# Unit 5's q and k in an attention and feed-forward kernel: transposed by a DMA instead of by TensorE

## The chip, the cores and the metric

The kernel runs on one NeuronCore of a Trainium2 chip. The metric is the device time of one execution in microseconds (us), taken as the median of several runs. The engines are TensorE (PE; its weight loads are listed as PEld), VectorE (DVE), ScalarE (ACT), GpSimd (POOL) and SyncE (SP). SP only issues DMAs here. The DMAs that SP issues run in queue q1, those that POOL issues in queue q0, those of ACT in q10; all share the core's 16 DMA engines.

## The reference

What is computed is attention with normalised q and k, followed by a feed-forward block with a leaky ReLU. Cut to what matters:

```python
batch, n_heads, seq, head_dim = 8, 12, 448, 64
n_tokens, d_model, d_ff = 3584, 768, 2048

def rmsnorm(x, g):
    rms = np.sqrt(np.mean(x * x, axis=-1, keepdims=True) + 1e-06)
    return x / rms * g

q_n, k_n = rmsnorm(q, g_q), rmsnorm(k, g_k)
scores = np.matmul(q_n, k_n.transpose(0, 1, 3, 2)) / np.sqrt(64)
scores = scores - np.max(scores, axis=-1, keepdims=True)
attn = np.exp(scores)
attn = attn / (np.sum(attn, axis=-1, keepdims=True) + 1e-09)
attn_out = np.matmul(attn, v)

x = attn_out.transpose(0, 2, 1, 3).reshape(3584, 768)
h = x @ w_in
out = np.maximum(0.01 * h, h) @ w_out
```

## The kernel before

**Units.** The 96 heads are worked off as 24 units of four heads, three units for a batch (`NU = 24`, `NQ = 3`, `QH = 4`). Each unit holds 4 x 448 rows of q, k and v, laid out on 128 partitions as `[128, 2, 7, 64]`.

**What one unit passes through**, with the lines that the profile names:

- `load` (L152): two DMAs of SP bring q and k as float32 into `raw` (three buffers each). `load_v` (L155): POOL brings v as float16 (four buffers).
- The squares, on POOL (`prep_sqp`, L179) for units 2 to 8, on ACT (L175) for the others; their sums on DVE (`prep_ssq`, L186); the inverse root as two small ACT instructions (`prep_rinv`, L191 and L192); the product with it on DVE, one instruction for q and one for k, into the float16 tile `n16`, of which there is one buffer (`prep_norm`, L198).
- The transpose of `n16` into `qkT` (three buffers), of which there are two kinds. With `prep_tr` (L205 to L212), TensorE multiplies seven 128 x 128 blocks with the identity (L210) into a PSUM bank, and DVE copies the bank to `qkT`; the copy of q multiplies by g on the way (`vcopy`, L822), the copy of k is plain (L824). With `prep_trd` (L215), one DMA of SP transposes q and k together, and DVE multiplies q by g in place afterwards (`prep_g`, L182).
- The scores (`qk`, L228): seven steps of four 64 x 64 matmuls over 448 columns, each step into a pair of PSUM banks. The step's exponential is one ACT instruction of 128 x 896 (`ex`, L243), which empties the pair. The first step also gives the unit's shift: a maximum on DVE (`shift_max`, L257 and L259), one matmul that spreads it over the partitions (`shift_mm`, L276) and two small DVE instructions (L277, L287).
- The product with v (`pv`, L403), the column sums (`zcol`, L340), some of whose terms DVE adds up first (`add_e`, L325), the copy out of PSUM (`pv_out`, L353 on DVE or L355 on ACT), the inverse of the sums on ACT (`zcol_ln`, L361, and `zcol_inv`, L366), which four small DMAs of SP spread over the partitions (L371), and the product with it (`xmul`, L381).

**The feed-forward block.** The two weight matrices are loaded by POOL's queue at the beginning (L131 for w_in; L134 for w_out, two DMAs of 1.5 MB each). While the units run, TensorE works off a queue of feed-forward items between a unit's groups of scores: products with w_in (`moe1`, L425), whose leaky ReLU is ACT's L419, and with w_out (L471 and, in a form with fewer products, L535). DVE forms the sums of weights for that form (`weight_sum`, L499).

**Order.** The order is written by hand and recorded as it stands (`manual_schedule`); no scheduler moves anything. Units 0 to 2 are written out one step after the other. From unit 3 on, a loop goes over the units `u` and, in each, over four groups `d`. A group issues its scores and exponentials, gathers a list of jobs, and then `fill` issues as many feed-forward items as a table says (`PLAN`), one job after each item, and the remaining jobs behind the last item. So a job's place in the list sets its place in each engine's queue. For unit u the groups do, for other units:

- group 0: `load(u + 4)`; up to u = 5 `prep_sqp(u + 3)`; up to u = 4 `load_v(u + 3)`. From u = 5 the load of v stands behind a one-element POOL copy that reads `qkT` of unit u + 1 (`gate_t_of`, L293).
- group 1: the sums of squares for u + 2.
- group 2: `prep_rinv` and `prep_norm` for u + 2, and, from u = 4, `prep_trd` for u + 2, so that unit 6 is the first that a DMA transposes.
- units 4 and 5 are transposed by `prep_tr`, in group 1 of unit 3 and in group 0 of unit 4.

A transpose of unit u + 2 must be read out of `n16` before the norm of unit u + 3 writes it, one unit later. The multiply by g of a unit that a DMA transposed is a job of group 1 in the unit before (`prep_g(u + 1)`, from u = 5).

**PSUM.** The eight banks are handed out from a list of free ones. Until unit 5, scores take pairs among banks 4 to 7 (two pairs), and single banks among 0 to 3 serve the feed-forward items, the sums and the transposes. From unit 5 all banks are shared, and a group takes three pairs.

Of the kernel before, what the change touches and what calls it, by code (L numbers as in the profile page):

```python
# [18 lines left out]
def kernel(  # L19
# [18 lines left out]
    NU = B * NQ  # L38
# [192 lines left out]
    def qk(u, steps):  # L231
        st[u]["sT"] = []
        for t in steps:
            sT = slot()
            score(u, t, (sT[:, 0], sT[:, 1]))
            st[u]["sT"].append((t, sT))
# [16 lines left out]
    def shift_max(u):  # L253
        s = st[u]
        sT = s["sT"][0][1]
        s["spare"] = sT[:, 0]
        nc.vector.tensor_reduce(s["spare"][:, 511:512], sT[:, :, 0:S], axis=AXL.XY, op=ALU.max)  # L257
        s["dg"] = small.tile([P, P], FP16, tag="dg", name="dg")
        nc.vector.tensor_tensor(s["dg"], ident16, s["spare"][:, 511:512].broadcast_to([P, P]), op=ALU.mult)  # L259
# [4 lines left out]
    def shift_mm(u):  # L264
        s = st[u]
        peak = s["spare"][:, 510:511]
        own = s.get("own")
        if own is not None:
            pb = own[:, :, S:S + 64]
            for x in range(2):  # L270
                nc.tensor.matmul(pb[:, x], onesp, s["dg"][:, 64 * x:64 * x + 64], start=True, stop=True)
            peak = small.tile([P, 1], FP32, tag="peak", name="peak")
            nc.vector.tensor_reduce(peak, pb, axis=AXL.XY, op=ALU.max)
        elif u > 0 and "zc" in st[u - 1]:
            pb = st[u - 1]["zc"][:, 2 * P:3 * P]
            nc.tensor.matmul(pb, onesp, s["dg"], start=True, stop=True)  # L276
            nc.vector.tensor_reduce(peak, pb, axis=AXL.X, op=ALU.max)  # L277
        else:
            if "pb" not in s:
                shift_bank(u)  # L280
            pb = s["pb"]
            nc.tensor.matmul(pb[:, 0:P], onesp, s["dg"], start=True, stop=True)
            nc.vector.tensor_reduce(peak, pb[:, 0:P], axis=AXL.X, op=ALU.max)
            if u >= 3:
                drop(pb)
        s["eb"] = small.tile([P, 1], FP32, tag="eb", name="eb")
        nc.vector.tensor_scalar(s["eb"], peak, -1.0, DELTA, op0=ALU.mult, op1=ALU.add)  # L287
# [44 lines left out]
    def zcol(u):  # L332
        s = st[u]
        s["zc"] = aux()
        ets = z_tiles(u)
        for i, e in enumerate(ets):
            for y in range(2):
                for a in range(2):
                    c = 32 * (2 * y + a)
                    nc.tensor.matmul(s["zc"][c:c + 32, 0:HS], onesr, e[:, a, HS * y:HS * y + HS],  # L340
                                     start=(i == 0), stop=(i == len(ets) - 1))

    def pv_slot(u):
        s = st[u]
        s["pslot"] = slot()
        s["pv"] = [s["pslot"][:, r] for r in range(2)]
        pv(u)
# [25 lines left out]
    def xmul_sb(u):  # L373
        xmul_pool(u, nc.vector)
# [76 lines left out]
    def flush(keep=0):  # L451
        kept = [p for p in pend if keep and (p[0] in (s1, s2, s3, s4) or hasattr(p[0], "waits") or keep == 5 and hasattr(p[0], "copies"))]
        now = [p for p in pend if p not in kept]
        pend[:] = kept
        for fn, args in now:
            fn(*args)
# [344 lines left out]
    def tripled(u):  # L801
        return 5 <= u < NU - 2

    def narrow(u):
        return 3 <= u < NU - 1
# [43 lines left out]
    with tc.manual_schedule():  # L849
# [208 lines left out]
        for u in range(3, NU):  # L1058
            for d in range(4):
                if u == 5 and d == 0:  # L1060
                    shared.append(u)
                if d > 0 or u > 3:
                    qk(u, (TRIPLES if tripled(u) else STEPS)[d])
                    if d == 0:
                        shift_max(u)
                        flush()
                        if u in (5, 6):
                            xmul_sb(u - 2)
                        if narrow(u - 1):
                            pv_slot(u - 1)  # L1070
                            zcol(u - 1)
                            shift_mm(u)
                            pv_out(u - 1)
                            if u < NU - 1:
                                zcol_ln(u - 1)
                                zcol_inv(u - 1)
                        else:
                            zsum_slot(u - 1)
                            pv(u - 1)
                            shift_mm(u)  # L1080
                            zinv(u - 1)
                    ex(u, 2)
                    if d == 0 and u == NU - 1:
                        zcol_ln(u - 1)
                if d == 2 and (u == 3 or ADDED.get(u, 0) > 3) and u < NU - 1:
                    add_e(u)
                    if u > 4:
                        xmul_sb(u - 1)
                jobs = []

                def job(fn, *args):
                    jobs.append(lambda: fn(*args))

                if d == 0:
                    if u == 3:
                        prep_norm(4)
                        gate(4)
                    elif not narrow(u - 1):
                        xmul(u - 1)
                    if u + 4 < NU:  # L1100
                        job(load, u + 4)
                    if u < 5:
                        load_v(u + 3)
                    if u < 6:
                        prep_sqp(u + 3)
                    if 5 <= u < NU - 3:
                        gate_t_of(u + 1)
                        load_v(u + 3)
                if d == 1 and narrow(u - 1) and not 5 <= u < 8 and ADDED.get(u, 0) < 4:
                    if u % 6 == 2:  # L1110
                        behind.append(u - 1)
                    elif u < NU - 2:
                        xmul_pool(u - 1)
                if u == NU - 1:
                    if d == 1:
                        job(zcol_inv, u - 1)
                if fed(u, d) and u > 3:
                    push(u // NQ - 1)
                if (u, d) in ((3, 1), (4, 0)):
                    for ti in range(2):  # L1120
                        prep_tr(u + 1, ti, VV)
                if u + 2 < NU:
                    if d == 1:
                        if ADDED.get(u) == 3 and u > 3:
                            job(lambda u: (prep_ssq(u + 2), add_e(u)), u)
                        else:
                            for ti in range(2):
                                job(prep_ssq, u + 2, ALL, (ti,))
                if d == 1 and 5 <= u < NU - 1:
                    job(prep_g, u + 1)  # L1130
                if u + 2 < NU:
                    if d == 2:
                        job(prep_rinv, u + 2)
                        if u == 6:
                            job(xmul_sb, u - 1)
                        for ti in range(2):
                            job(prep_norm, u + 2, ALL, (ti,))
                        if u > 3:
                            job(prep_trd, u + 2)
                if d == 1 and 4 <= u < 8:  # L1140
                    job(weight_sum, u - 4, 0)
                if d == 0 and 5 <= u < 9:
                    job(weight_sum, u - 5, 1)
                if d == 1 and u == NU - 2:
                    job(xmul_sb, u - 1)
                    job(add_e, u)
                if u == NU - 2 and d == 0:
                    for n, tile_ in ((1, (raws, "rq", 3)), (2, (raws, "rk", 3)), (3, None), (4, (prep_p, "sq", 3))):
                        job(win_sum, n, 1, tile_)
                    for n in (3, 1, 2, 4):  # L1150
                        job(x_sum, LATE, n)
                if u == NU - 1 and d == 3:
                    job(add_e, u)
                    job(xmul_sb, u - 1)
                if d == 3 and 6 <= u < NU - 3:
                    for ti in range(2):
                        job(prep_sq, u + 3, ALL, (ti,))
                if st[u]["sT"]:
                    n = 1 if d == 1 and u % 6 == 2 else 0
                    jobs[n:n + 1] = [also(lambda: ex(u), *jobs[n:n + 1])]  # L1160
                fill(u, d, jobs)
# [39 lines left out]
```

## Time and profile before

| | |
|---|---|
| median of 3 runs | 409.06 us (408.88 to 409.59) |
| the profiled execution | 408.8 us, of which the span of the profile is 406.9 us |
| granted TensorE clock | 1.00 throughout |
| TensorE busy | 396.7 us (97%) |
| VectorE busy | 311.3 us (76%) |
| ScalarE busy | 303.9 us (75%) |
| GpSimd busy | 70.6 us (17%) |
| DMA transposes (L215) | 18, median 4.0 us from issue to landing, the longest 6.6 us |
| transposes on TensorE through `prep_tr` (L210) | 42 matmuls, between 33.7 and 56.6 us |
| w_out (L134) | issued at 30.8 and 33.3 us, landed 25.5 to 31.4 us later |
| shift of units 3 and 4 begins (L257) | at 38.93 and 54.11 us |

The span runs from the first to the last instruction of the profile; the time of an execution holds a little more. A line of the timeline gives an instruction's start and length in us, its engine, its source line, its operation, what it writes and reads, and in square brackets how long its engine stood idle before it and what ended that. Busy shares are averages over a start, 21 units and an end of different kinds. PE's ends are modelled, so that consecutive matmuls overlap a little in the timeline. The DMA view lists packets, megabytes and the time that the packets took as a share of 16 engines, for each queue in a stretch of time.

### The profile page before, as it was taken

Reading aid. Unit: us, or ns where it says so; the run is one execution under the profiler, and the core shown is the slowest. Engines: PE = TensorE matmul, PEld = TensorE weight load, DVE = VectorE, ACT = ScalarE, POOL = GpSimd, SP = SyncE. Lnnn points to the kernel's source line nnn. Section 1 sums busy time; section 2 is a strip of 40 time slices with the busy share of each in tenths; the row PEclk is TensorE's granted clock in tenths of the full one; section 3 lists DMA queues with packets and bytes.
Section 4 is the critical chain, followed back from the end, with each engine's and each line's share of the span. In section 5 each row is a group of like instructions: output and inputs, shape, how many; then the busy total and the mean of one; then the engine's idle time right before and its main releaser. Section 6 shows DMA issues by size and latency. Waiting matters only on the chain.

```text
span 406.9 us, 9527 instructions
## 1 busy us (share of the span) xinstructions
PE 396.7 (97%) x3876; PEld 225.0 (55%) x3876; DVE 311.3 (76%) x482; ACT 303.9 (75%) x474; POOL 70.6 (17%) x88
## 2 busy tenths in 40 slices
PE   8999999999999999999999999999999999999996
PEld 7665454555455544555455544555455557559963
DVE  5888999988879665886679756787679889567672
ACT  5998877788977699778978689868987667743600
POOL 1787432200120200120011200020002200000000
PEclk9999999999999999999999999999999999999999
DMA  6999999999455887478563795777732470022023
GB/s 197 276 235 251 240 235 246 236 223 213 96 156 110 239 216 117 135 198 192 137 159 66 226 218 116 187 178 170 177 72 49 122 169 0 20 68 79 0 57 99
DMA packets 72527, 62.87 MB, mean 154 GB/s; under 512 B 36389, under 2 KB 67621, under 8 KB 72485
## 3 DMA queue, kind: packets, MB, share of 16 engines
q1 hardware_dynamic: 61888, 50.08, 46.3%
q0 software_dynamic: 10272, 11.80, 18.8%
q8 instruction: 30, 0.49, 0.5%
q10 hardware_dynamic: 324, 0.39, 0.3%
q14 instruction: 13, 0.10, 0.1%
HBM read 45.61 MB, written 11.01 MB: 139 GB/s over the span
## 4 chain that ended last, share of the span: by engine, by line
PE 87%; DVE 2%; issue 0%; DVEq 0%
PE banks L425 29%; PE banks L535 25%; PE banks L228 9%; PE banks L471 8%; PE banks L669 6%; PE banks L403 6%; PE banks L340 3%; PE banks L276 1%; DVE banks L257 1%; DVE ost L542 1%; PE banks L210 0%; PE banks L433 0%; DVE xt L412 0%; DVE dg L259 0%; PE banks L313 0%
## 5 line engine op out<-in xcount | busy, mean ns | idle before, releaser
L243 ACT ACTIVATE et<-banks,eb 128x896 f16<-128x896 f32 x168 | 160.6, 1008 | 22.8 <-PE banks L228 22.1
L425 PE MATMUL banks<-xt,win 128*128 128x448 f16 x612 | 122.2, 353 | 0.0
L425 PEld LDWEIGHTS <-win 128*128 128x128 f16 x612 | 57.6, 98 | 56.2 <-issue 6.9
L419 ACT ACTIVATE gt<-banks 128x448 f16<-128x448 f32 x104 | 55.2, 551 | 9.1 <-PE banks L425 7.6
L186 DVE TENSOR_REDUCE ssq<-sq 128x14 f32<-128x896 f32 (+2 forms) x49 | 50.3, 1058 | 0.8 <-ACT sq L175 0.8
L228 PE MATMUL banks<-qkT 64*64 64x448 f16 x672 | 49.0, 361 | 1.6 <-DVE qkT L824 0.8
L535 PEld LDWEIGHTS <-sa 128*128 128x128 f16 x352 | 33.4, 98 | 26.1 <-issue 5.1
L535 PE MATMUL banks<-tw,sa 128*128 128x384 f16 x264 | 46.9, 326 | 0.0
L542 DVE TENSOR_TENSOR ost<-banks,ost 128x384 f32<-128x384 f32 x55 | 30.4, 553 | 13.2 <-PE banks L535 12.3
L257 DVE TENSOR_REDUCE banks<-banks 128x1 f32<-128x896 f32 x24 | 26.3, 1098 | 15.1 <-PE banks L228 11.1
L403 PE MATMUL banks<-et,vt 64*64 64x448 f16 x672 | 36.9, 349 | 0.0
L535 PEld LDWEIGHTS <-gt 128*128 128x128 f16 x264 | 25.5, 98 | 18.2 <-issue 1.7
L198 DVE TENSOR_TENSOR n<-rq,rinv 128x896 f16<-128x896 f32 (+2 forms) x25 | 33.1, 1328 | 1.9 <-ACT rinv L192 1.9
L471 PE MATMUL banks<-wout,gt 128*128 128x384 f16 x192 | 33.7, 326 | 0.0
L228 PEld LDWEIGHTS <-qkT 64*64 64x64 f16 x672 | 16.6, 105 | 29.1 <-issue 21.8
L535 PE MATMUL banks<-wout,gt 128*128 128x384 f16 x176 | 32.4, 326 | 0.0
L293 POOL COPY gate_t<-qkT 128x1 f16<-128x1 f16 x16 | 4.0, 251 | 152.3 <-DMA qkT<-n 152.3
L198 DVE TENSOR_TENSOR n<-rk,rinv 128x896 f16<-128x896 f32 (+2 forms) x26 | 26.1, 1012 | 0.0
L403 PEld LDWEIGHTS <-vt 64*64 64x64 f16 x672 | 20.0, 107 | 10.0
L471 PEld LDWEIGHTS <-gt 128*128 128x128 f16 x192 | 18.0, 98 | 13.7 <-issue 2.9
L325 DVE TENSOR_TENSOR ea<-et 128x896 f16<-128x896 f16 x14 | 10.0, 714 | 18.2 <-ACT et L243 18.2
L381 POOL TENSOR_TENSOR xt<-x,rz 128x896 f16<-128x896 f32 x8 | 16.6, 2077 | 32.3 <-DMA rz<-zs 26.0
(109 smaller groups left out, 492.4 us busy)
## 6 DMA issues: line engine op xcount, KB each, us to landing
rq<-in_q_dram SPq DMA_DIRECT2D x24, 448.0 KB, 5.2
rk<-in_k_dram SPq DMA_DIRECT2D x24, 448.0 KB, 6.0
out_dram<-ost SPq DMA_DIRECT2D x52, 192.0 KB, 3.0
rz<-zs SPq DMA_DIRECT2D x80, 112.0 KB, 3.6
vt<-in_v_dram POOLq DMA_DIRECT2D x24, 224.0 KB, 5.3
win<-in_moe_w_in_dram POOLq DMA_DIRECT2D x8, 384.0 KB, 14.7
wout<-in_moe_w_out_dram POOLq DMA_DIRECT2D x2, 1536.0 KB, 28.4
out_dram<-ost SPq DMA_DIRECT2D x4, 96.0 KB, 2.1
```

The source lines that it names most:

```text
L186: nc.vector.tensor_reduce(buf(u, "ssq")[:, ti, :, c[0]:c[1]], buf(u, f"sq{ti}")[:, :, c[0]:c[1]], axis=AXL.X, op=ALU.add)
L198: nc.vector.tensor_tensor(buf(u, "n16")[:, ti, c[0]:c[1]].rearrange("p s a d -> p a s d"), src[:, :, c[0]:c[1]], buf(u, "rinv")[:, ti, :, ...
L228: nc.tensor.matmul(banks[a][64 * r:64 * r + 64, 0:S].rearrange("p (t x) -> p t x", t=NS), kT(u, r, a, t), qT(u, r, a), start=True, stop=True)
L243: nc.scalar.activation(s["et"][:, t], sT[:, :, 0:S], AF.Exp, bias=s["eb"], scale=1.0)
L257: nc.vector.tensor_reduce(s["spare"][:, 511:512], sT[:, :, 0:S], axis=AXL.XY, op=ALU.max)
L403: nc.tensor.matmul(s["pv"][r][64 * a:64 * a + 64, 0:S], vts[u % NV][64 * r:64 * r + 64, a, t], s["et"][64 * r:64 * r + 64, t, a], start=(t ...
L419: nc.scalar.activation(dst, src, AF.Prelu, bias=0.0, scale=1.0, alpha=0.01)
L425: nc.tensor.matmul(hps[:, 0:S], win16[:, kt // 2, kt % 2, ts(ft, P)], xt[:, kt // 2, kt % 2], start=(kt == 0), stop=(kt == KT - 1))
L471: nc.tensor.matmul(op2[:, 0:HC], gt[:, ft, ds(col(t), P)], wout16[:, ft, ds(HC * half, HC)], start=(i == 0), stop=(i == FT - 1))
L535: nc.tensor.matmul(bank[:, 0:HC], a[:, f], b[:, f], start=(first and f == 0), stop=(f == HF - 1), skip_group_check=not first)
L542: nc.vector.tensor_tensor(dst, g[name][:, 0:HC], src, op=ALU.add)
L669: nc.tensor.matmul(bank[:, HX * i:HX * i + HX].rearrange("p (t x) -> p t x", t=NS), w, x[:, kt], start=start, stop=(kt == HK - 1), skip_gr ...
```

## The change

Unit 5 is no longer transposed by TensorE in group 0 of unit 4. Its transpose is issued as a DMA, as a last job of group 2 of unit 3, and its multiply by g becomes the first job of group 2 of unit 4. The later units keep their order.

```diff
@@ -1116,7 +1116,7 @@
                 if fed(u, d) and u > 3:
                     push(u // NQ - 1)
-                if (u, d) in ((3, 1), (4, 0)):
+                if (u, d) == (3, 1):
                     for ti in range(2):
                         prep_tr(u + 1, ti, VV)
@@ -1126,7 +1126,7 @@
-                if d == 1 and 5 <= u < NU - 1:
+                if d == (2 if u == 4 else 1) and 4 <= u < NU - 1:
                     job(prep_g, u + 1)
                 if u + 2 < NU:
                     if d == 2:
                         job(prep_rinv, u + 2)
                         if u == 6:
                             job(xmul_sb, u - 1)
                         for ti in range(2):
                             job(prep_norm, u + 2, ALL, (ti,))
-                        if u > 3:
-                            job(prep_trd, u + 2)
+                        job(prep_trd, u + 2)
```

In the order of the instructions, TensorE loses 14 transposes (L210, two banks of seven) between unit 4's L276 and the next L425. DVE loses one L822 and one L824 of 128 x 896 there, and gains one L182 of 128 x 896 ahead of unit 6's norm. SP gains one transpose between the loads of unit 7 and the four copies of unit 3's L371. On ACT, the small pair L191 and L192 for unit 6 moves behind the second L419 of its group. The functions that the change calls in new places stand unchanged:

```python
def prep_g(u):
    nc.vector.tensor_scalar(buf(u, "qkT")[:, 0], buf(u, "qkT")[:, 0], gcol, None, op0=ALU.mult)

def prep_trd(u):
    nc.sync.dma_start_transpose(
        out=buf(u, "qkT").rearrange("p t s x -> p (t s) x"),
        in_=buf(u, "n16").rearrange("p t s a d -> p (t s a d)"))
```

## The prediction

> **What bounds the kernel now.** I read the page first, then the chain of waits, then the timeline of units 3 to 5, then the DMA view of short stretches.
>
> ```profile
> span 406.9 us, 9527 instructions
> PE 396.7 (97%) x3876; PEld 225.0 (55%) x3876; DVE 311.3 (76%) x482; ACT 303.9 (75%) x474; POOL 70.6 (17%) x88
> DMA  6999999999455887478563795777732470022023
> ```
>
> TensorE is busy for 97% of the span, so whatever it no longer does, or waits for, shows in the end. The DMA digits are 9 or more from slice 2 to slice 10 (10 to 102 us): the change puts its transfer into the fullest stretch. In the chain, the transposes that go are one entry:
>
> ```profile
> 56.06 0.78 PE banks L210 x14
> 56.85 1.14 PE banks L425 x6
> 57.98 0.56 PE banks L228 x8
> ```
>
> What stands around it in the timeline (start, length):
>
> ```profile
> 55.84 0.23 PE L276 MATMUL banks<-dg,onesp 128*128 128x128 f16 x1
> 56.44 0.36 ACT L361 ACTIVATE zs<-banks 128x224 f32<-128x224 f32 x1 [2.15 <-DVE banks L277]
> 57.12 0.99 ACT L243 ACTIVATE et<-banks,eb 128x896 f16<-128x896 f32 x1
> 57.51 0.68 DVE L822 TENSOR_SCALAR qkT<-banks,gcol 128x896 f16<-128x896 f16 x1
> 58.10 0.61 DVE L824 COPY qkT<-banks 128x896 f16<-128x896 f16 x1
> ```
>
> L276 makes unit 4's shift, and ACT starts on unit 4 only after it. This is ahead of the transposes and does not move. The first exponential ends at 57.12 + 0.99 = 58.11.
>
> **TensorE's part.** Removed: 14 transposes, 0.78 us of the chain. The six matmuls of L425 then end near 57.2. The scores behind them (L228 x8) need two pairs of PSUM banks: one is emptied by DVE's L353 (56.51, 1.08 us: 57.59), the other by that exponential, at 58.11. Today the second four scores begin near 58.2, so they gain about 0.1 us, and the rest of the 0.78 us becomes a wait. ACT has no room to follow either: from 56.44 to 66.43 its timeline shows one idle moment, 0.17 us. Gain on the path: 0.1 us, at most 0.78. Two PSUM banks less are taken in turn, so the built program uses other banks in units 4 and 5 and the same ones from unit 6; none of the new waits names a late reader, so I cost it at 0.
>
> **DVE's and ACT's part.** Removed: L822 and L824, 57.51 to 58.63, 1.12 us. Added: one multiply L182, 0.44 us (median of its 18; 1.09 where POOL's squares run beside it, but POOL idles from 61.5 to 69.4). ACT's small pair for unit 6 (L191, L192, 0.5 us) comes behind the second prelu of the group instead of ahead of it, so unit 6's norm can start at about 64.8, against 64.92 now: cost 0. DVE reaches the new multiply near 64.0: it is four adds behind, and the last add waits for an exponential that ends at 63.30.
>
> **The DMA's part.** Added: one transpose of 448 KB on SP's queue, when unit 5's norm ends (53.00 + 1.08 = 54.1). It stands ahead of four copies that are issued at 57.24. Issuing the next unit's took SP 2.63 us:
>
> ```profile
> 57.24 2.58 SPq L371 DMA_DIRECT2D rz<-zs  x4
> ...
> 67.07 2.63 SPq L215 DMA_TRANSPOSE qkT<-n  x1
> ```
>
> So 54.1 + 2.63 = 56.8, before 57.24: SP delays nobody, with 0.4 us to spare. No POOL gate follows this transpose. In q1's rings, though, the four copies (needed at 68.45 by L381) and unit 8's loads now lie behind it.
>
> What is late if it lands late: the multiply, and behind it in DVE's order the norm of unit 6 and the maximum of unit 5, on which TensorE's shift waits.
>
> ```profile
> 64.92 1.08 DVE L198 TENSOR_TENSOR n<-rq,rinv 128x896 f16<-128x896 f32 x1
> 65.92 1.08 DVE L198 TENSOR_TENSOR n<-rk,rinv 128x896 f16<-128x896 f32 x1
> 67.11 1.10 DVE L257 TENSOR_REDUCE banks<-banks 128x1 f32<-128x896 f32 x1
> 68.65 0.23 PE L276 MATMUL banks<-dg,onesp 128*128 128x128 f16 x1
> ```
>
> From a landing: 0.05 to start, 0.40 for the multiply, 2.08 for the norms (64.92 to 67.00), 0.07 to L257, so L257 starts 2.6 us after it. Today it starts at 67.11. Loss = landing - 64.5, and 0 before that. TensorE's own path (scores of unit 5 right after the multiply, then pv, 1.32 us, and 0.3 to 0.4 of sums) is shorter than DVE's.
>
> When does it land? The trace has no transpose against a full software queue; each later one has its rings nearly to itself. I bound it from the rows of four stretches: 50 to 54, 57 to 61, 64.2 to 67 and 58 to 71.1 us, one after the other (packets, MB, share of time):
>
> ```profile
> q0 software_dynamic: 328, 0.50, 68.1%
> q1 hardware_dynamic: 325, 0.55, 43.0%
> ...
> q0 software_dynamic: 543, 0.83, 114.5%
> ...
> rz<-zs SPq DMA_DIRECT2D x4, 112.0 KB, 7.4
> ...
> q0 software_dynamic: 358, 0.30, 66.1%
> q1 hardware_dynamic: 361, 0.42, 51.8%
> ...
> q0 software_dynamic: 1444, 1.63, 71.6%
> ```
>
> q0 carries w_out and v, q1 is SP's. Where both have work they move the same number of packets, 328 to 325 and 358 to 361, whatever their sizes. From 57 to 61 q1 moves nothing although L371 was issued at 57.24: a first packet takes some 3.8 us to appear beside a full q0. So unit 5's transpose begins at 54.1 + 3.8 = 57.9, and then q0 still has 1444 packets. A transpose alone, in the stretch 92.4 to 95:
>
> ```profile
> q1 hardware_dynamic: 1846, 0.52, 107.5%
> ```
>
> some 1,800 small packets in 2.6 us, 710 per us. Lower bound: q0 yields; 57.9 + 2.6 + 0.5 (last packet to landing: issued at 91.32, landed 4.0 later) = 61.0, no loss. Upper side: packet for packet, the transpose is not through until q0 has run out. Those 1444 packets take at least 1.63 MB / 211 GB/s (q0 alone from 57 to 61) = 7.7 us and at most 1444 / 128 per us (358 in 2.8 us) = 11.3 us. The other 348 packets take 0.5 us, the landing 0.5. Sum: 66.6 to 70.2, and up to 71 if the slowest ring decides, as q0 itself ran until 71.0. I take packet for packet, because both rows with two busy queues show it, and 69.0, a little above the middle, since the small packets are not free to q0 either. Loss 69.0 - 64.5 = 4.5 us; the 0.1 us of TensorE is lost in that wait.
>
> [...] The rows of two plain transfers agree with one record a turn; no row of this case shows a transpose's turn.
>
> **Sum.** This execution: 406.9 us of span, 1.9 us around it, 408.8. Plus 4.5: span 411.4, 413.3. The median of the runs, 409.06, lies 0.26 above the profiled one: 413.5.
>
> **Rivals.**
>
> First, the transfer is hidden: the transpose gets more than one packet a turn and lands before 64.5. For it: about 10 us between norm and multiply, and a transpose alone needs 4.0. Against it: the equal counts above. Then only TensorE's 0.1 us stays: 409.0, not slower. It decides from one point, landing at 64.5.
>
> Second, the change does what it removes: all of 0.78 us comes off the path, 408.3. It would need an early landing and the second pair of banks free by 57.4, while the exponential that empties it ends at 58.11 and hangs on L276, which does not move. Even whole, it is 0.19%.
>
> Third, half late: two or three packets a turn, landing 65.3 to 66.5, loss 0.8 to 2.0: 410 to 411.
>
> Fourth, later than my upper side: the engines wait for each other within the transpose, or TensorE loses its clock in the gap. All stretches of this trace show the granted clock at 1.00, so no row prices it; with a landing at 71.5 the loss is 7, 416. [...]
>
> **How the numbers follow.** Packet for packet with a loss of 2 to 7 us: 0.58, own range 411.1 to 416. Hidden: 0.24. Whole gain: 0.08. Half late: 0.05. Later still: 0.05. About 0.2% (0.8 us) is what a measurement of this kernel tells from no change. Slower 0.58 + 0.05 + 0.05 = 0.68; of the hidden case 0.22 is within the bound and 0.02 beyond, as is the whole gain: same 0.22, faster 0.10. The range starts at the hidden case, 408.8, and ends at 416; outside it lie the whole gain and the last case, some 0.15.
>
> **What would show it.** Right: DVE idle ahead of L182 near 64 us, ended by the DMA qkT<-n; that transpose landing 12 us or more after issue, against 4.0 to 6.6 of the others; TensorE idle near 66.6 and again ahead of the next L276; from there every line later by the same amount. In any case: no L210 after 47 us and a wait of L228 near 57.6. Wrong: L182 near 64 without idle time, and L276 of unit 5 at 68.6 or before. Equal packet counts on q0 and q1 from 58 us on would prove the step on turns, 1,800 packets on q1 while q0 moves a few hundred would refute it.

## The result and the profile after

The changed kernel takes 416.32 us (416.04 to 416.52, four runs) against 409.03 for the kernel before in the same comparison: 1.0177 times as long, 95% interval 1.0162 to 1.0191. The forecast was 413.5 and its range ended at 416.0, so the direction was right and the loss was 7.3 us where 4.5 had been forecast. The profiled execution is one of 416.39 us. (Further down, three executions that were disturbed as a whole, of `a1_gate_v`, of `b1_no_tr` and of the kernel before, at 2,253, 803 and 1,405 us, are left out.)

First the page of the changed kernel: its span, the busy times, and the chain of waits by engine and line.

```profile
span 414.4 us, 9499 instructions
PE 398.1 (96%) x3862; PEld 224.9 (54%) x3862; DVE 309.5 (75%) x481; ACT 303.8 (73%) x474; POOL 70.5 (17%) x88
...
PE 83%; DMA 4%; DVE 2%; issue 0%; DVEq 0%
```

TensorE has 14 instructions fewer and is busy for 1.4 us longer. A DMA now holds 4% of the chain. The chain in order of time, from 54 us, says which one:

```profile
54.11 0.18 PE banks L403
54.29 16.95 DMA qkT<-n
71.24 0.03 issue
71.26 0.46 DVE qkT L182
71.73 0.14 issue
71.86 0.59 PE banks L228 x4
```

The transpose is issued at 54.29 and lands at 71.24. The multiply waits for it, and TensorE waits for the multiply. The timeline of the same stretch (start, length; in brackets the idle time ahead and what ended it):

```profile
63.46 0.62 DVE L325 TENSOR_TENSOR ea<-ea,et 128x896 f16<-128x896 f16 x1 [0.18 <-ACT et L243]
64.36 2.44 PE L425 MATMUL banks<-xt,win 128*128 128x448 f16 x12
71.26 0.45 DVE L182 TENSOR_SCALAR qkT<-qkT,gcol 128x896 f16<-128x896 f16 x1 [7.18 <-DMA qkT<-n]
71.63 1.08 DVE L198 TENSOR_TENSOR n<-rq,rinv 128x896 f16<-128x896 f32 x1
73.64 1.09 DVE L257 TENSOR_REDUCE banks<-banks 128x1 f32<-128x896 f32 x1
74.97 2.08 DVE L381 TENSOR_TENSOR xt<-x,rz 128x896 f16<-128x896 f32 x1
75.68 0.29 PE L276 MATMUL banks<-dg,onesp 128*128 128x128 f16 x1
79.59 0.66 PE L471 MATMUL banks<-wout,gt 128*128 128x384 f16 x3
```

DVE is through with its adds at 64.08 and stands until 71.26. The shift of unit 5 (L276) begins at 75.68 where it began at 68.65, and the second group of L471 at 79.59 where it began at 72.10. This execution's unit 4 ran 0.12 us later (its L276 at 55.96 against 55.84), so the loss is 6.9 us at the shift and 7.4 us at L471; the spans differ by 7.5. The whole loss arises here, between 64 and 80 us.

Two smaller things are in it. One begins at SP: its four issues of L371 take longer (the first alone 4.84 us), so unit 8's loads go out later, POOL's squares, which wait for these loads, begin later, and L381 now runs beside them and takes 2.08 us instead of 1.08. First the kernel before, then the changed one:

```profile
57.24 2.58 SPq L371 DMA_DIRECT2D rz<-zs  x4
59.92 0.54 SPq L152 DMA_DIRECT2D rq<-in_q_dram  x1
69.41 1.68 POOL L179 TENSOR_TENSOR sq<-rq 128x896 f32<-128x896 f32 x1 [7.95 <-DMA rq<-in_q_dram]
72.10 2.77 PE L471 MATMUL banks<-wout,gt 128*128 128x384 f16 x16
```

```profile
57.37 6.93 SPq L371 DMA_DIRECT2D rz<-zs  x4
64.40 0.57 SPq L152 DMA_DIRECT2D rq<-in_q_dram  x1
74.42 1.68 POOL L179 TENSOR_TENSOR sq<-rq 128x896 f32<-128x896 f32 x1 [13.95 <-DMA rq<-in_q_dram]
```

The other is that the granted clock falls. The view of stretches gives busy time and number of instructions by engine, then the clock, the DMA share and GB/s:

```profile
57.80:69.80 12.00, 8.87 (x60) 3.76 (x59) 5.89 (x7) 9.51 (x16) 2.11 (x2) 1.00 1.26 182
69.80:76.70 6.90, 4.84 (x49) 2.35 (x50) 5.40 (x6) 0.00 (x0) 1.68 (x1) 0.51 1.09 257
```

Last the DMA view of the changed kernel, from 58 to 64 us (packets, megabytes, share of 16 engines):

```profile
q0 software_dynamic: 709, 1.03, 94.2%
q1 hardware_dynamic: 670, 0.17, 21.6%
```

709 packets against 670: the transpose's packets of 256 bytes and the software queue's, 626 of them of 1,536 bytes and 73 of 896, pass in nearly equal number. (That they pass one by one, and not several at a time on both sides, is shown under `d1_fetch` for the last engine there.)

### The profile page after: what moved, and what is told of

The parts are those of the page before. It is cut to its first block, busy times and chain, and to the rows that moved or that the text cites. A ratio compares the mean times of both kernels' runs of the same rounds, so it can differ in the third digit from the quotient of the medians.

```text
span 414.4 us, 9499 instructions
## 1 busy us (share of the span) xinstructions
PE 398.1 (96%) x3862; PEld 224.9 (54%) x3862; DVE 309.5 (75%) x481; ACT 303.8 (73%) x474; POOL 70.5 (17%) x88
## 4 chain that ended last, share of the span: by engine, by line
PE 83%; DMA 4%; DVE 2%; issue 0%; DVEq 0%
PE banks L425 26%; PE banks L535 25%; PE banks L228 8%; PE banks L471 8%; PE banks L669 6%; PE banks L403 6%; DMA qkT<-n 4%; PE banks L340 2%; PE banks L276 1%; DVE banks L257 1%; DVE ost L542 1%; PE banks L433 0%; DVE xt L412 0%; PE banks L210 0%; DVE dg L259 0%
## 5 line engine op out<-in xcount | busy, mean ns | idle before, releaser
L425 PE MATMUL banks<-xt,win 128*128 128x448 f16 x612 | 122.2, 353 | 0.0
L425 PEld LDWEIGHTS <-win 128*128 128x128 f16 x612 | 57.6, 98 | 56.2 <-issue 6.9
L419 ACT ACTIVATE gt<-banks 128x448 f16<-128x448 f32 x104 | 55.1, 550 | 9.3 <-PE banks L425 7.7
L228 PE MATMUL banks<-qkT 64*64 64x448 f16 x672 | 49.3, 362 | 7.2 <-DVE qkT L182 5.1
L257 DVE TENSOR_REDUCE banks<-banks 128x1 f32<-128x896 f32 x24 | 26.3, 1097 | 17.2 <-PE banks L228 14.1
L403 PE MATMUL banks<-et,vt 64*64 64x448 f16 x672 | 38.2, 359 | 0.0
L228 PEld LDWEIGHTS <-qkT 64*64 64x64 f16 x672 | 16.6, 105 | 34.9 <-issue 22.1
L471 PE MATMUL banks<-wout,gt 128*128 128x384 f16 x192 | 34.2, 329 | 0.0
L471 PEld LDWEIGHTS <-gt 128*128 128x128 f16 x192 | 18.1, 99 | 14.0 <-issue 3.2
L361 ACT ACTIVATE zs<-banks 128x224 f32<-128x224 f32 x20 | 7.3, 365 | 20.2 <-DVE banks L277 19.8
```

Source lines behind the costliest of these rows:

```text
L228: nc.tensor.matmul(banks[a][64 * r:64 * r + 64, 0:S].rearrange("p (t x) -> p t x", t=NS), kT(u, r, a, t), qT(u, r, a), start=True, stop=True)
L403: nc.tensor.matmul(s["pv"][r][64 * a:64 * a + 64, 0:S], vts[u % NV][64 * r:64 * r + 64, a, t], s["et"][64 * r:64 * r + 64, t, a], start=(t ...
L419: nc.scalar.activation(dst, src, AF.Prelu, bias=0.0, scale=1.0, alpha=0.01)
L425: nc.tensor.matmul(hps[:, 0:S], win16[:, kt // 2, kt % 2, ts(ft, P)], xt[:, kt // 2, kt % 2], start=(kt == 0), stop=(kt == KT - 1))
L471: nc.tensor.matmul(op2[:, 0:HC], gt[:, ft, ds(col(t), P)], wout16[:, ft, ds(HC * half, HC)], start=(i == 0), stop=(i == FT - 1))
```

## The experiments

All times are set against the kernel before in the same comparison, 409.03 to 409.1 us. The theory to be tested is the prediction's: the transpose's packets take turns with the software queue's, and the loss is what its landing is late for DVE.

**Was there anything to gain?** `b1_no_tr` is the kernel before without unit 5's transposes; unit 5's scores read a part of w_in instead.

```diff
+                if (u, d) == (4, 0):
+                    st[5]["qkT"] = win16[:, 0, 0, 0:2 * NS * P].rearrange("p (t s x) -> p t s x", t=2, s=NS)
-                if (u, d) in ((3, 1), (4, 0)):
+                if (u, d) == (3, 1):
```

> The kernel before without any transpose of unit 5: no products with the identity, no copies, no DMA, no multiply by g; unit 5's scores read a part of w_in in place of its transposed q and k. Theory 1 (of TensorE's 0.78 us all but 0.1 becomes a wait for a pair of PSUM banks): 408.95 us, and a wait of L228 near 57.6. Theory 2 (the 0.78 us come off the path): 408.3 us.

Measured: 0.9997 times before, 0.9987 to 1.0006. Its timeline:

```profile
56.34 0.23 PE L276 MATMUL banks<-dg,onesp 128*128 128x128 f16 x1
58.15 0.90 PE L228 MATMUL banks<-qkT 64*64 64x448 f16 x8 [0.45 <-DVE x L353]
69.16 0.23 PE L276 MATMUL banks<-dg,onesp 128*128 128x128 f16 x1
```

From shift to shift it is 12.82 us, and 12.81 in the kernel before. TensorE's 0.78 us turns into a wait for a pair of banks at L228. Even a transpose that costs nothing at all gains nothing here. So, with the other work in this order, no placing of the DMA can beat the kernel before by more than the interval leaves.

**Half a transpose.** `a3_half` sends q alone by the DMA; k goes through seven products with the identity.

```diff
-                        job(prep_trd, u + 2)
+                        job(prep_trd, u + 2, 1 if u == 3 else 2)
...
-            out=buf(u, "qkT").rearrange("p t s x -> p (t s) x"),
+            out=buf(u, "qkT")[:, 0:n].rearrange("p t s x -> p (t s) x"),
...
+                if (u, d) == (4, 0):
+                    prep_tr(u + 1, 1, VV)
```

> The changed kernel with unit 5's q alone transposed by the DMA (128 x 7 x 128, half the packets) and its k by seven products with the identity, as before. Theory 1 (packet for packet): 896 packets at 113 a us from 58.0 end at 65.9, landing near 66.5, loss 2.0 us, no fall of the clock: 411.1 us. Theory 2 (a transpose gets through only when q0 has run out, whatever its length): landing near 70 to 71, 415.5 us or more.

Measured: 410.92 us, 1.0044 (1.0030 to 1.0059). DVE's wait at L182 shrinks from 7.18 to 1.11 us. Half the packets cost 1.9 us of the 7.3, far less than half, as a loss that counts from one moment (64.5 us by the forecast) demands.

**Fewer neighbours.** `a1_gate_v` and `c1_gate_v` are one kernel, run twice, the second time for its profile: v of units 5, 6 and 7 is fetched only when unit 5's transpose has landed.

```diff
         pv(1, 4, NS)
-        load_v(5)
...
-                    if u < 5:
-                        load_v(u + 3)
+                    if u == 4:
+                        gate_t_of(5)
+                        for w in (5, 6, 7):
+                            load_v(w)
```

> The changed kernel, with POOL's loads of v for units 5, 6 and 7 held back until unit 5's transpose has landed, so that behind 58 us only w_out stands in q0. Theory 1 (the transpose gets one packet for each packet of q0): w_out's some 650 packets left at 58 us go in pairs at 113 a us, until 63.8; the other 1,140 packets of the transpose at 710 to 780 a us, until 65.4; landing near 66.0, loss 66.0 - 64.5 = 1.5 us, TensorE waits too short for its clock to fall: 410.5 us. Theory 2 (this transpose is slow for a reason of its own, its place on SP or the rings' waiting for each other, not for q0's backlog): landing near 71 as before, 416.3 us.

> The changed kernel with the loads of v for units 5, 6 and 7 held back until unit 5's transpose has landed (the same kernel as a1_gate_v; this time for its profile). T1 (the transpose's packets go one for one with the software queue's, so with fewer of those it lands earlier): landing near 66 instead of 71.2, DVE's wait at L182 below 2.5 us instead of 7.2, time 410.3 to 411.5. T2 (the transpose is slow by itself and the neighbours do not matter): landing stays near 71, time near 416.3.

Measured: 1.0051 (1.0033 to 1.0070) and 1.0059 (1.0038 to 1.0080); the ten runs of the second lie between 409.49 and 413.29, and the profile is of the one at 409.49. Its timeline, and its DMA view from 58 to 62 and from 62 to 65 us:

```profile
65.14 0.46 DVE L182 TENSOR_SCALAR qkT<-qkT,gcol 128x896 f16<-128x896 f16 x1 [1.00 <-DMA qkT<-n]
68.98 0.22 PE L276 MATMUL banks<-dg,onesp 128*128 128x128 f16 x1
```

```profile
q0 software_dynamic: 449, 0.69, 93.8%
q1 hardware_dynamic: 455, 0.12, 21.9%
...
q1 hardware_dynamic: 1556, 0.51, 97.9%
q0 software_dynamic: 101, 0.13, 24.3%
```

From 58 to 62 us, while q0 has work, q1 moves 114 packets per us; from 62 to 65, as q0 runs dry with its last 101, 519. The transpose lands at 65.1, six us earlier than in the changed kernel though not a byte of it differs, and the shift comes only 0.16 us late (68.98, of an execution whose unit 4 ran 0.17 us later). So the neighbours set the landing. Why the other runs of this kernel take up to 4 us more wasn't seen in a profile.

`c2_half_gate` joins both edits (the gate reads q's part).

> The changed kernel with both reliefs: only q by the DMA (k by seven products with the identity again), and v of units 5, 6 and 7 held back until it has landed. T1 (only the landing against DVE's free moment, some 64.5, counts): landing 62 to 64, DVE's wait at L182 near zero, time 408.8 to 409.4. T2 (a DMA transpose costs the kernel something at this place even when it is on time, by its packets in front of rz and of the loads, or by the lower clock): 410.2 or more.

Measured: 410.56 us, 1.0043 (1.0026 to 1.0060); five runs at 409.7 to 410.0 and five at 411.2 to 412.1. The profile is of one at 411.81. The landing and the time that the first theory gave are both missed:

```profile
66.03 0.45 DVE L182 TENSOR_SCALAR qkT<-qkT,gcol 128x896 f16<-128x896 f16 x1 [1.28 <-POOL gate_t L293]
69.73 2.53 DVE L381 TENSOR_TENSOR xt<-x,rz 128x896 f16<-128x896 f32 x1
69.87 0.22 PE L276 MATMUL banks<-dg,onesp 128*128 128x128 f16 x1 [0.82 <-DVE dg L259]
```

Half the transpose lands at about 65.8, where 62 to 64 was expected: q0 still moves 247 packets between 62 and 66 us here. What keeps it busy longer than in `c1_gate_v` stays open. The time lies in the second theory's range, but the transpose was not on time, so this run doesn't test that theory; `g1_unread` below does. The lines show how a small delay grows: the shift is 0.9 us late, but L381 then runs beside POOL's squares, 2.53 us instead of 1.08, and the second group of L471 is 2.1 us late.

**The stall.** In the changed kernel the packets of both queues stop for a while. From 66.3 to 67.6 us the view counts

```profile
q0 software_dynamic: 58, 0.05, 90.7%
q1 hardware_dynamic: 57, 0.01, 80.6%
```

where the 1.3 us before had 211 and 218: few packets, but their time adds up to 171% of the 16 engines, and single ones take up to 1.27 us. Just ahead lies a fetch of 16 KB of instructions (65.36, 1.38 us). `d1_fetch` cuts 80 filler matmuls at the start into 160 smaller ones, so that the fetches fall at 57.0 and 74.3 us.

```diff
-        for x in range(n):
-            nc.tensor.matmul(bank[:, P:2 * P], onesp, onesp, start=True, stop=True)
+        w = 64 if n in (32, 48) else P
+        for x in range(n * P // w):
+            nc.tensor.matmul(bank[:, P:P + w], onesp, onesp[:, 0:w], start=True, stop=True)
```

> The changed kernel with 80 of the start's filler matmuls 128x128 cut into 160 of 128x64 (the same work in more instructions, so that TensorE's 16 KB fetches of instructions come at other times). T1 (the fetch at 65.4 stops both queues for 1.26 us of the landing): the stall is gone from the transpose's stretch or moves with the fetch; without it the landing is near 70.0, DVE's wait near 6.0, time 415.0 to 415.4. T2 (the stall is the transpose's own, or the software queue's): a stall of 1.2 us stands where no fetch is, landing 71.2, time 416.3.

Measured: 415.80 us, 1.0169 (1.0154 to 1.0184). Its counts from 66.1 to 67.4, and from 68.5 to 70 us:

```profile
q0 software_dynamic: 216, 0.18, 85.6%
q1 hardware_dynamic: 266, 0.07, 38.4%
...
q1 hardware_dynamic: 168, 0.09, 105.4%
q0 software_dynamic: 19, 0.01, 5.9%
```

The stall has gone with the fetch, as the first theory says, but DVE's wait is 6.79 us, only 0.39 shorter, and the time is above the 415.0 to 415.4 expected. In the last 1.5 us only 187 packets move. Part of those in q1 are already of rz, which stands next in it. From 69.05 to 69.82 us the view counts

```profile
DMA packets 60, 0.05 MB, mean 62 GB/s; under 512 B 9, under 2 KB 60, under 8 KB 60
q0 software_dynamic: 9, 0.01, 5.7%
```

and the trace's records of single packets show what these are: eight packets of q0 (896 bytes) and eight of the transpose (256 bytes) in strict turn, a pair every 0.095 us. That is the pace of one engine: 216 of q0's packets in 1.3 us on 16 engines, as counted above, make 0.096 us each. So one engine is left, and once its last packet of q0 is through, the transpose's last ten follow within 0.14 us, the last at 69.95; the transpose lands at 70.53. The landing is that of the slowest engine, and the stall was partly hidden behind this tail. Why that engine has more left than the others stays open.

**The clock.** `a2_warm` puts 64 unneeded 128 x 128 matmuls ahead of unit 5's first scores.

```diff
+                if u == 5 and d == 0:
+                    kept = list(free)
+                    wb = aux()
+                    warm(64, wb)
+                    free[:] = kept
                 if d > 0 or u > 3:
                     qk(u, (TRIPLES if tripled(u) else STEPS)[d])
```

> The changed kernel with 64 matmuls more (128 x 128, into a free bank, read by nobody) ahead of unit 5's first scores, so that TensorE is busy until some 70.3 us instead of 66.8. Theory 1 (the clock's fall costs about 0.9 us on top of the late landing: 0.5 because TensorE's sums at half clock end after DVE's shift, 0.45 on the 16 products behind it): granted clock 1.00 throughout, L276 0.5 us nearer to the landing, 415.4 us. Theory 2 (the late landing and DVE's chain behind it are the whole loss, the clock hits nothing on the path): clock 1.00, 416.3 us.

Measured: 415.72 us, 1.0159 (1.0144 to 1.0173), with the granted clock at 1.00 from 66 to 78 us. That is 0.60 us less than the changed kernel, but 0.30 us of it is in DVE's wait at L182 (6.88 us instead of 7.18), which ends with the landing. Counted from L182, the shift comes 0.58 us earlier than in the changed kernel (3.84 us behind it instead of 4.42), the second group of L471 only 0.22 (8.11 instead of 8.33). So the fall of the clock costs 0.6 us at most, and more likely 0.2 to 0.3.

**A transpose that nobody waits for.** `g1_unread` keeps the products with the identity and adds a second transpose of the same size, from w_in to a part of `tw` that is overwritten later.

```diff
+    def unread(u):
+        twf = tw[:, 3].rearrange("p h c -> p (h c)")[:, 0:2 * NS * P]
+        nc.vector.tensor_copy(twf[:, 2 * NS * P - 1:2 * NS * P], buf(u, "n16")[:, 1, NS - 1, 1, D - 1:D])
+        nc.sync.dma_start_transpose(out=twf.rearrange("p (s x) -> p s x", x=P), in_=win16[:, 0, 0, 0:2 * NS * P])
...
-                        if u > 3:
-                            job(prep_trd, u + 2)
+                        job(prep_trd if u > 3 else unread, u + 2)
```

> The kernel before, its products with the identity kept, with one more DMA transpose of the same size issued on SP's queue after unit 5's normalization (behind a one-column copy on DVE), from a part of w_in into a part of tw that is written over later; nobody reads it. T1 (all of the loss is DVE's wait for the landing): 408.9 to 409.4. T2 (the packets themselves cost the neighbours: rz, the load of unit 8 and w_out come later): 410 or more, with L381 or L257 waiting for a DMA.

Measured: 414.36 us, 1.0141 (1.0118 to 1.0163), 5.3 us more than before. The theory as it stood falls: without any wait for the transpose most of the loss is still there. The timeline names the reader (what is L381 elsewhere is L386 in this kernel):

```profile
68.47 0.29 DVE L264 TENSOR_TENSOR dg<-ident,banks 128x128 f16<-128x128 f16 x1
72.62 1.09 DVE L386 TENSOR_TENSOR xt<-x,rz 128x896 f16<-128x896 f32 x1 [3.86 <-DMA rz<-zs]
73.63 0.29 DVE L282 TENSOR_REDUCE banks<-banks 128x1 f32<-128x128 f32 x1
```

The four copies rz stand behind the transpose in SP's queue and land at about 72.6, needed at 68.8. Behind L386 in DVE's order stands L282 (L277 before), and for that ACT's exponentials and then TensorE wait. In the changed kernel this second wait is invisible: DVE reaches L381 only at 74.97, when rz is there.

**Order in the queue, or load on the engines?** Three kernels answer with a plain copy of 1,792 pieces of 256 bytes. Their base, `p0_base`, is the kernel before without any DMA transpose: units 6 and later read a part of w_in, without the multiply by g; the first 66 us are as before. `p1_copy_sp` issues the copy where `g1_unread` does, `p2_copy_act` issues it on ACT's queue.

```diff
+    def unread(u):
+        dst = tw[:, 3].rearrange("p h c -> p (h c)")[:, 0:2 * NS * P]
+        nc.vector.tensor_copy(dst[:, 2 * NS * P - 1:2 * NS * P], buf(u, "n16")[:, 1, NS - 1, 1, D - 1:D])
+        src = win16[:, 0].rearrange("p r n -> p (r n)")[:, 0:28 * P].rearrange("p (c x) -> p c x", x=2 * P)[:, :, 0:P]
+        nc.sync.dma_start(dst.rearrange("p (c x) -> p c x", x=P), src)
```

> The kernel before without any of its DMA transposes (units 6 and later: their scores read a part of w_in instead, and the multiplies by g are gone); unit 5 keeps its products with the identity, so that the first 66 us are those of the kernel before. The base of p1, p2 and p4. Both theories: close to before, 407.0 to 409.2, since TensorE bounds it.

> p0 with an unread plain copy of 1792 pieces of 256 bytes, from w_in to a part of tw, in the place and on the queue of g1's unread transpose (SP's, ahead of rz). T1 (rz stands behind it in one queue): L381 waits for rz by 3 to 4 us, p0 plus 4 to 5.5 us. T2 (it takes something that only a DMA transpose does, its engines waiting for each other): p0 plus less than 1 us.

> p0 with the same unread copy issued on ACT's queue, in ACT's idle time ahead of L361, so that rz stands behind nothing. T1 (order in the queue makes rz late): rz lands before 68.4, p0 plus 0 to 0.4. T2 (three queues in turn slow rz anyway): p0 plus 1 us or more, L381 waits for rz.

Measured: `p0_base` 409.94 us (409.72 to 410.28), a little above the kernel before and above the 409.2 expected, for a reason that wasn't looked for; `p1_copy_sp` 414.39, 4.45 more; `p2_copy_act` 410.06, 0.1 more. The first timeline line is of `p1_copy_sp`, the second of `p2_copy_act`:

```profile
72.18 1.09 DVE L382 TENSOR_TENSOR xt<-x,rz 128x896 f16<-128x896 f32 x1 [3.57 <-DMA rz<-zs]
```

```profile
68.33 1.08 DVE L382 TENSOR_TENSOR xt<-x,rz 128x896 f16<-128x896 f32 x1
```

And the DMA view of `p2_copy_act` from 62 to 64 us:

```profile
q0 software_dynamic: 219, 0.23, 67.6%
q1 hardware_dynamic: 221, 0.17, 34.3%
q10 hardware_dynamic: 221, 0.06, 13.5%
```

Three queues, 219, 221 and 221 packets. The same bytes at nearly the same time cost 4.45 us ahead of rz in its queue and nothing measurable in another, where q1 keeps a third of the packets and rz is in time. So it is the order in the queue, not the load. Behind the copy SP's four issues of rz also take longer, 7.61 us in `p1_copy_sp` against 2.58 in `p2_copy_act`, the first alone 4.82. How much of rz's delay is this late issue, and how much its place in the queue, wasn't separated. That a transpose acts here as the copy does is argued, from the like losses of `g1_unread` and `p1_copy_sp`; no transpose that nobody reads was run on ACT's queue or behind rz.

**The multiply's wait alone.** In `p4_wait_act`, also on the base `p0_base`, unit 5's q and k come from such a copy on ACT's queue, and L182 waits for it; rz stands behind nothing.

```diff
+                        if u == 4:
+                            copied(5)
...
+        dst = buf(u, "qkT").rearrange("p t s x -> p (t s x)")
...
+        nc.scalar.dma_start(dst.rearrange("p (c x) -> p c x", x=P), src)
```

> p0 with the multiply's wait alone: unit 5's q and k come from such a copy of w_in on ACT's queue, no products with the identity, and DVE's multiply by g (L182) waits for it where the changed kernel waits for the transpose; rz stands behind nothing. T1 (the multiply's wait and rz's lie side by side, either alone costs most of the loss): DVE waits 4 us or more at L182, p0 plus 4.5 to 7.5. T2 (rz sets the loss): p0 plus less than 2.

Measured: 419.15 us, 9.2 more than the base. L182 waits 8.58 us, and L382 for no DMA:

```profile
73.19 0.45 DVE L182 TENSOR_SCALAR qkT<-qkT,gcol 128x896 f16<-128x896 f16 x1 [8.58 <-DMA qkT<-win]
...
76.89 1.08 DVE L382 TENSOR_TENSOR xt<-x,rz 128x896 f16<-128x896 f32 x1
```

That is more than the 7.5 us allowed for: ACT issues the copy at 56.27, some 1.5 us later in the unit than SP does, and it takes 16.9 us from there as well. But the two waits are told apart now: the multiply's alone costs more than rz's alone (9.2 and 4.45), and they lie side by side, so that the later one counts. By this, freeing rz would not save the changed kernel. That is argued: the changed kernel itself with its transpose on ACT's queue wasn't run, nor with POOL's squares kept away from L381.

## Why the prediction was right in kind and short in size

- *TensorE's part, 0.1 us of 0.78.* Right as far as can be told: in `b1_no_tr` the gain is 0.03%, and 0.13% (0.5 us) at the end of the interval.
- *SP's part.* Right for the issue: at 54.29, 1.42 us (2.63 taken), first packet at 58.2 (57.9 taken). "SP delays nobody" was wrong: behind the transpose the four issues of rz took 6.93 us instead of 2.58, and unit 8's loads went out 4.4 us later in the unit.
- *DVE reaches the multiply near 64.0.* Right: 64.08.
- *Packet for packet.* Right: 709 to 670, 219 to 221 to 221, and one by one on the last engine of `d1_fetch`. That no row of before showed a transpose's turn was true; these records (the packets that the DMA view counts) show it, one of 256 bytes for one of 896, a pair every 0.095 us.
- ***When it lands* is the step that failed**: "69.0, a little above the middle" of 66.6 to 70.2, "and up to 71 if the slowest ring decides". It landed at 71.24, above that whole range. The sum spread q0's packets evenly over the engines and gave them 7.7 to 11.3 us; the tail, in which the slowest engine ends, had only that last remark. In `d1_fetch`, without the stall, all but 80 of the transpose's 1,792 packets are through at 68.5, near the 69.0, and the landing comes 2.0 us later, at 70.5 (0.5 of this was in the sum). The row of the kernel before was in hand: there q0's 1444 packets took 13.1 us, until 71.1. The stall at 66.3 us, which no row of before showed, adds 0.4 us.
- *Loss = landing - 64.5.* It gives 6.7 us, and the shift was 6.9 late. DVE's part of it held: L257 starts 2.4 us after the landing (2.6 taken). But TensorE's own path was not the shorter one: at half the clock its sums (L340) end at 75.74, after DVE's L259 at 75.05, and the shift stands behind them. The 0.5 us that follow, up to L471, come beside a longer L381; that was not in the sum. `a2_warm` puts the clock's share of the whole at 0.6 at most.
- *"0 before that"* does not follow. The copies rz were named as lying behind the transpose and then given no price: alone they cost 4.45 to 5.3 us. In the changed kernel they hide behind the multiply, so the number didn't suffer, but the account was incomplete.
- *The rivals.* Hidden, half late and whole gain are refuted by the wait. The fourth, a landing at 71.5 and 416 us, is what came in number. Of what it named, a wait of the engines for each other was not shown: the stall of the transpose, whose cause is open, was worth 0.4 us, and the clock 0.6 at most; most of the lateness is the tail, which it didn't name. On the clock, TensorE's last product ended at 66.80, it stood idle for 5.1 us, until 71.86, and the granted clock was at half (0.50) from 69.82 to 76.65, so it fell 3.0 us after the last product. `a2_warm` puts the price at 0.6 us at most. That most of the stretch waits for DVE anyway would explain so little; this is argued.

## What to carry to other kernels

The DMA that shared its engines with a busy queue here was through when the slowest engine was: in `d1_fetch` all but 80 of its 1,792 packets at 68.5 us, and the landing at 70.53. So price such a DMA by the other queue's last packet, not by a mean rate. Then list everything behind it in its own queue with the moment at which each is needed: here two waits lay side by side (9.2 us alone in `p4_wait_act`, 4.45 in `p1_copy_sp`), and the profile of the changed kernel showed only the later. And before moving work off the busiest engine, ask what the engine would wait for next; here 0.78 us of TensorE's work was worth nothing.

## What the runs showed of the hardware

- Two queues that both had work moved nearly equal numbers of packets of unlike size: 709 (1,536 and 896 bytes) and 670 (256) in the changed kernel from 58 to 64 us, 449 and 455 in `c1_gate_v` from 58 to 62. So did three: 219, 221 and 221 in `p2_copy_act` from 62 to 64. Where one engine was left, in `d1_fetch` from 69.05 to 69.82 us, packets of 896 and 256 bytes passed strictly one by one, a pair every 0.095 us.
- During a DMA transpose, both queues stalled soon after a 16 KB instruction fetch: single packets took up to 1.27 us from 66.3 in the changed kernel (fetch at 65.36), 1.27 us from 65.8 in `a2_warm` (64.91; 139 GB/s from 66 to 69 us, 199 from 69 to 72) and 1.09 us from 64.7 in `g1_unread` (63.75; q0 and q1 moved 101 and 111 packets in the 1.3 us from 64.6). In the changed kernel the held packets all ended between 67.56 and 67.66. Beside the plain copy of `p1_copy_sp` a fetch of 0.95 us at 63.6 stopped nothing: q0 and q1 moved 206 and 204 packets in the 1.3 us from 63.5. A fetch is not the only occasion: in the kernel before, ten packets of unit 6's transpose that began between 69.61 and 70.41, with no fetch of 16 KB near (63.69 and 73.34), all ended between 71.20 and 71.23, as q0 ran out. That the stall belongs to the transpose is inferred from these runs; what causes it was not shown.
- DVE's 128 x 896 multiply of float32, 1.08 us alone, took 2.08 and 2.53 us (changed kernel, `c2_half_gate`) when it began beside POOL's squares; in both it ended 0.95 us after the square did.
- The granted clock stayed at half (0.50) for 6.83 us in the changed kernel, from 69.82 to 76.65, 2 us of that idle, and came back while TensorE was working on L471 (from 75.76).
